# Folding a Fourier transform's first stage into sums and differences of token pairs, in four 64 x 64 float32 products instead of three split products

## The chip, the core and the metric

The kernel runs on one core of one Trainium2 chip. The metric is the device time of one execution in microseconds (us). The engines are TensorE (PE, with its weight loads shown as PEld), VectorE (DVE), ScalarE (ACT), GpSimd (POOL) and SyncE (SP, which here issues nearly all DMA transfers).

## The reference

```python
X = np.fft.rfft(x, axis=1)                       # x: (8, 2496, 256), float32
Y = X * (filt_r + 1j * filt_i)[None]
x = np.fft.irfft(Y, n=2496, axis=1).reshape(8 * 2496, 256)
logits = x @ phi                                 # phi: (256, 32): 8 experts of 4 slots
d = softmax(logits, over all tokens)
slot_input = (d.T @ x).reshape(8, 4, 256)
slot_out = relu(slot_input[e] @ w1[e]) @ w2[e]   # for each expert e, hidden size 1024
out = softmax(logits, over the slots) @ slot_out
```

All eight batches are filtered along their 2496 tokens; then a soft mixture of experts runs over all 19968 tokens together.

## The kernel before

The transform of length 2496 is split as 39 x 64. The **first stage** is a transform of length 39 over tokens that lie 64 apart. Three such groups of tokens stand on 117 partitions of one tile, and two of these sets make a *unit* of 512 columns; a batch has 11 units (`NH`). As a matrix the stage is `w1q`, 117 x 120: cosines and sines for 20 frequencies (`NT`; the other 19 follow by symmetry), for three groups side by side, so that a third of it is not zero. For batch 0 a unit is one float32 matmul (line 323). For batches 1 to 7 the product is split: `split_x` rounds the tokens to the short float kind `float32r` on ACT (line 310, tile `xh`) and takes the remainder on POOL (line 311, `xl`), and `s1_unit` adds three one-pass products, `w1h` by `xh`, `w1l` by `xh` and `w1h` by `xl` (line 327). The result is copied out of PSUM (line 331 on ACT; in batch 0 every second one by line 329 on DVE) to a tile `at` and written to a scratch tensor in HBM, `a_dram`. PSUM has two buffers of one bank for it.

The **second stage** works in *slots*, ten to a batch (`CPB`), 80 in all. `load_ash` brings two frequencies of the scratch back with another order of axes (tile `ash`, five buffers). `x_unit` multiplies by the length-64 transform (line 357, four float32 matmuls) and by the filter tables `ff_t` on DVE and POOL (lines 371 to 375). Two slots later `t_unit` transposes the result (line 383), copies it to `y` on ACT (line 385) and, every second slot, forms the logits in the frequency domain (line 394, strips of 32 columns). Batches are gathered in five groups; when a group is complete, the generator `chain` takes its logits back to tokens and through the soft-max statistics and sums (line 417 and around it), two steps in each slot.

Order: `slot_of` spreads the first-stage units of batches 1 to 7 over 65 slots (`SPAN`), after `EARLY` units that are done before slot 0. In slot n the program issues loads, `split_next(n + 1)` prepares the units of the next slot, `x_unit` runs, then `s1_unit` for this slot's units, then `t_unit` of slot n - 2. A scheduler orders the instructions of each engine from the program's order and priorities; `behind` pins chosen instructions in a queue's written order, among them SP's transfers up to slot 24 (`PIN`). `keep_warm` issues matmuls on zeros during the fill.

After the last slots the last two chains, the experts' layers (lines 910 and 928, strips of 32 columns) and the output products (line 966, strips of 32 rows) follow, and the result is written.

The main loop's order in the code, cut:

```python
for n in range(NS + LT):
    ...
        load_to(n)
        ...
        split_next(n + 1)
        x_unit(*divmod(n, CPB))
    for b, u in at_slot.get(n, ()):
        s1_unit(b, u)
    ...
        t_unit(b, c)
    ...
    hop_slot(n)
```

## Time and profile before

| what | value |
|---|---|
| median of 3 timed runs | 402.03 us (398.9 to 402.43) |
| profiled execution, its own time | 398.26 us |
| its span in the profile | 396.3 us |
| PE busy | 362.1 us, 91% |
| PE weight loads busy | 278.9 us, 70% |
| DVE busy | 264.2 us, 67% |
| ACT busy | 212.6 us, 54% |
| POOL busy | 200.8 us, 51% |
| DMA | 109.08 MB, mean 275 GB/s |

Shares are of the span of one execution. Matmuls are pipelined and float32 matmuls show two records each, so the sum of their durations is more than the time that PE needs; starts of records tell the pace. Lines are named as L327; in a row of groups stand engine, operation, tile written and read, shapes, count, busy time, mean duration and the idle time of the engine before them with what ended it.

### The profile page before, as it was taken

The page shows a single profiled execution, that of the slowest core. Times are in us where ns is not written, and L with a number is a line of the kernel's source. Part 1 is how long each engine was busy: PE and PEld are TensorE (multiplying, and loading weights), DVE is VectorE, ACT ScalarE, POOL GpSimd, SP SyncE. Part 2 cuts the span into 40 slices and gives each one's busy share as a digit, 9 for nine tenths or more (in the row PEclk, how much of TensorE's full clock was granted, in tenths as well). Part 3 has the DMA queues.
Part 4 walks back from the last instruction along what each step waited for, and adds up shares of the span by engine and source line. Part 5 has one row for each costly group of instructions (what it writes and reads, how often), then busy time and mean ns, then how long its engine had stood idle before and what let it go on. Part 6 is the DMA issues. An engine that isn't in the chain of part 4 may idle for free.

```text
span 396.3 us, 11436 instructions
## 1 busy us (share of the span) xinstructions
PE 362.1 (91%) x4569; PEld 278.9 (70%) x4569; DVE 264.2 (67%) x460; ACT 212.6 (54%) x453; POOL 200.8 (51%) x229
## 2 busy tenths in 40 slices
PE   8967889999999999999998999999999899999960
PEld 2455767887878776887887778888767544777850
DVE  1215998779789973967899355899644653588640
ACT  2356656675666946665675634347235431577430
POOL 0157688797668674856774615663421112361000
PEclk9999999999999999999998999999999999999555
DMA  8999999899889866976897783454529998299997
GB/s 293 316 291 368 395 374 373 288 318 341 261 274 305 288 212 207 291 250 171 283 328 215 200 271 104 130 147 134 170 70 380 364 249 278 111 413 421 418 414 296
DMA packets 54010, 109.08 MB, mean 275 GB/s; under 512 B 5362, under 2 KB 25970, under 8 KB 51782
## 3 DMA queue, kind: packets, MB, share of 16 engines
q1 hardware_dynamic: 53412, 108.01, 80.5%
q8 instruction: 36, 0.59, 0.6%
q10 hardware_dynamic: 546, 0.35, 0.3%
q14 instruction: 16, 0.13, 0.1%
HBM read 65.60 MB, written 42.74 MB: 273 GB/s over the span
## 4 chain that ended last, share of the span: by engine, by line
PE 61%; DVE 15%; DMA 13%; ACT 3%; issue 3%; POOL 2%; SPq 1%; DVEq 0%; ACTq 0%; POOLq 0%
PE x L357 14%; PE s L327 9%; PE t L383 7%; DMA out<-ob 5%; PE l L394 4%; PE s L417 4%; DMA ff_t<-in_ff 3%; DMA xt<-in_x 3%; PE v L417 3%; PE dd L417 2%; DVE t L372 2%; PE u L417 2%; PE lg L417 2%; DVE yt L371 2%; DVE yt L374 2%
## 5 line engine op out<-in xcount | busy, mean ns | idle before, releaser
L311 POOL TENSOR_TENSOR xl<-xt,xh 117x512 fp32r<-117x512 f32 x77 | 104.4, 1367 | 37.6 <-ACT xh L310 35.5
L357 PE MATMUL x<-cst_t,ash 128*128 128x128 f32 x640 | 90.2, 281 | 2.9 <-issue 2.3
L357 PEld LDWEIGHTS x<-cst_t,ash 128*128 128x128 f32 x640 | 81.6, 192 | 13.3 <-issue 7.5
L375 POOL TENSOR_TENSOR yt<-yt,t 128x256 f32<-128x256 f32 x80 | 65.4, 818 | 45.5 <-DVE t L372 35.9
L371 DVE TENSOR_TENSOR yt<-x,ff_t 128x512 f32<-128x512 f32 x80 | 54.7, 683 | 27.4 <-PE x L357 25.3
L385 ACT COPY y<-t 128x512 f32<-128x512 f32 x80 | 46.1, 591 | 35.5 <-PE t L383 33.2
L331 ACT COPY at<-s 120x512 f32<-120x512 f32 x83 | 48.5, 587 | 26.2 <-PE s L327 15.1
L310 ACT CAST xh<-xt 117x512 fp32r<-117x512 f32 x77 | 46.3, 623 | 23.4 <-PE s L327 12.6
L372 DVE TENSOR_TENSOR t<-x,ff_t 128x512 f32<-128x512 f32 x80 | 54.2, 678 | 0.0
L383 PE MATMUL t<-cst_t,yt 128*128 128x128 f32 x320 | 48.8, 277 | 4.8 <-POOL yt L375 4.1
L374 DVE TENSOR_TENSOR yt<-yt,t 128x256 f32<-128x256 f32 x60 | 45.3, 766 | 0.8
L383 PEld LDWEIGHTS t<-cst_t,yt 128*128 128x128 f32 x320 | 36.7, 141 | 12.7 <-POOL yt L375 7.2
L327 PE MATMUL s<-xh,w1h 117*120 117x512 f32 x77 | 35.9, 466 | 3.3 <-ACT at L331 2.1
L966 PE MATMUL out<-so,st 32*128 32x256 f32 x468 | 35.6, 337 | 2.0 <-ACT ob L971 1.0
L966 PEld LDWEIGHTS out<-so,st 32*128 32x128 f32 x468 | 30.7, 222 | 6.2 <-ACT ob L971 3.1
L327 PE MATMUL s<-xl,w1h 117*120 117x512 f32 x77 | 31.7, 416 | 0.3 <-POOL xl L311 0.3
L374 POOL TENSOR_TENSOR yt<-yt,t 128x256 f32<-128x256 f32 x20 | 15.1, 754 | 32.6 <-DVE t L372 19.9
L971 DVE COPY ob<-out 128x512 f32<-128x512 f32 (+1 forms) x40 | 25.0, 669 | 8.5 <-DMA out<-ob 5.5
L327 PE MATMUL s<-xh,w1l 117*120 117x512 f32 x77 | 30.4, 395 | 0.0
L971 ACT COPY ob<-out 128x512 f32<-128x512 f32 (+1 forms) x40 | 21.7, 583 | 14.8 <-DMA out<-ob 7.5
L394 PE MATMUL l<-yt,phi_t 128*32 128x128 f32 x640 | 27.5, 280 | 0.1
L394 PEld LDWEIGHTS l<-yt,phi_t 128*32 128x32 f32 x640 | 15.8, 109 | 9.1 <-issue 4.5
(107 smaller groups left out, 474.0 us busy)
## 6 DMA issues: line engine op xcount, KB each, us to landing
ash<-a_dram SPq DMA_DIRECT2D x80, 256.0 KB
a_dram<-at SPq DMA_DIRECT2D x80, 240.0 KB
xt<-in_x SPq DMA_DIRECT2D x35, 512.0 KB
out<-ob SPq DMA_DIRECT2D x17, 1024.0 KB
w<-in_wx SPq DMA_DIRECT2D x42, 256.0 KB
w<-in_wx SPq DMA_DIRECT2D x6, 512.0 KB
x_t<-in_x SPq DMA_DIRECT2D x5, 512.0 KB
ff_t<-in_ff SPq DMA_DIRECT2D x10, 256.0 KB
```

Source lines behind the costliest of these rows:

```text
L311: pool_e.tensor_tensor(out=xl, in0=xs, in1=xh.bitcast(F32), op=ALU.subtract)
L327: pe.matmul(ps, w, xx, start=(n == 0), stop=(n == 2))
L331: act.copy(at, ps)
L357: pe.matmul(ps[:, 2 * k + dh].rearrange("q r c -> q (r c)"), ash[:, k, dh * P : (dh + 1) * P], C("b1" if t0 + k else "b0"), start=True, st ...
L371: dve.tensor_tensor(out=yt, in0=ps, in1=frv, op=ALU.mult)
L372: dve.tensor_tensor(out=t2, in0=ps[:, :, ::-1, :], in1=fiv, op=ALU.mult)
L374: add.tensor_tensor(out=yt[:, :, 1, :], in0=yt[:, :, 1, :], in1=t2[:, :, 1, :], op=ALU.add)
L375: pool_e.tensor_tensor(out=yt[:, :, 0, :], in0=yt[:, :, 0, :], in1=t2[:, :, 0, :], op=ALU.subtract)
L383: pe.transpose(pt[:, k, dh, :], yt[:, c % 2, 2 * k + dh].rearrange("q r c -> q (r c)"), ident)
L394: pe.matmul(pl[32 * j : 32 * j + 32, :], phi_t[:, dh, :], yt[:, j // 2, 2 * (j % 2) + dh].rearrange("q r c -> q (r c)"), start=(dh == 0), ...
L417: line(pe.matmul(*a, **k))
L966: nc.tensor.matmul(prs[k][:, mm, :], sts[n][q, hs, c0 : c0 + P], so[q, ho], start=(i == 0), stop=(i == 2))
```

## The change

The tokens s and 39 - s of a group meet the same cosine and opposite sines. The change has the host lay such pairs side by side (`token_layout`, 19 pairs and the unpaired token 0, 20 rows; three groups on 60 of 64 partitions, and two sets of these on the two halves of the tile), and the kernel forms their sum and difference (`fold_x`, tile `eo`), on POOL for batches 1 to 7 and on DVE for batch 0 and the first two pieces of batch 1. The stage is then a cosine product of the sums and a sine product of the differences, each 64 x 64 for one half of the partitions: four float32 matmuls, one in each quarter of the array, into one PSUM tile of two banks. They get a high priority, so that they stand side by side; so do those of line 394. Work goes in *pieces* (`PIECE`) of two units, one of a single unit first: six to a batch. One copy on ACT takes a piece out of PSUM (two instructions in batch 0, where three pools of PSUM take turns). The scratch has cosine and sine parts as its outer axis, each piece is written by two transfers, and the constants of the second stage are ordered to match (`a1`). The split matrices `w1h` and `w1l`, the cast on ACT and the remainder on POOL are gone. `EARLY` goes from 4 units to 1, the loads of batch 1 move behind batch 0's writes, and the warm-up matmuls are placed anew. The PSUM pool of the stage is closed after its last piece and opened again with two buffers of one bank for the steps behind it.

```diff
@@ -46,8 +46,11 @@
 XC = 4
 XB = 3
-AB = 5
-EARLY = 4
+AB = 4
+EARLY = 1
+PIECE = ((0, 1), (1, 3), (3, 5), (5, 7), (7, 9), (9, 11))
+NU = len(PIECE)
+HR = 20
 SPAN = 65
 ASH = 5
 LT = 2
@@ -55,10 +58,9 @@
 RT = 1
 PR = 2
 FB = 1
-WM = 1
-WK = 2
+WM = 2
+WK = 1
 PIN = 24
-FIRST = (0, 2, 6, 10, 14, 18, 22)
 PA = 6
 YB = 34
 TAIL = (
@@ -73,7 +75,7 @@
 def slot_of(b, u):
-    k = (b - 1) * NH + u - EARLY
+    k = (b - 1) * NH + PIECE[u][1] - 1 - EARLY
     return k * SPAN // ((BATCH - 1) * NH - EARLY) if k >= 0 else -1
@@ -116,20 +118,26 @@
         blocks.append((name, a))
     w1f = w1.reshape(N1, QR)
-    w1q = np.zeros((PK, N1, PK, QR))
+    fold = np.zeros((2, HR, 2, NT))
+    fold[0, :, 0] = w1[0:HR, 0]
+    fold[1, 1:, 1] = w1[1:HR, 1]
+    w1q = np.zeros((2, 64, 2, 64))
     w1d = np.zeros((PK, N1, 2, PK, 2, NT // 2))
     cq = np.zeros((PK, QR, PK, N1))
     for j in range(PK):
-        w1q[j, :, j] = w1f
+        sl = slice(HR * j, HR * j + HR)
+        w1q[:, sl, 0, sl] = fold[0, :, 0]
+        w1q[:, sl, 1, sl] = fold[1, :, 1]
         cq[j, :, j] = w1f.T
         w1d[j, :, :, j] = w1.reshape(N1, 2, 2, NT // 2).transpose(0, 2, 1, 3)
-    w1q = w1q.reshape(KR, QP)
-    put("b0", b0.reshape(P, P))
-    put("b1", b1.reshape(P, P))
+    w1q = w1q.reshape(P, P)
+    put("b0", b0.transpose(1, 0, 2, 3).reshape(P, P))
+    put("a1", b1.transpose(1, 0, 2, 3).reshape(P, P))
     put("id", np.eye(P))
     put("sgn", sgn.reshape(NT // 2, P))
     put("m0", inverse(bh))
     put("m1", inverse(b1))
+    put("b1", b1.reshape(P, P))
     put("bh", bh.reshape(P, P))
     put("w1d", w1d.reshape(KR, 2 * PK * NT))
     put("cq", cq.reshape(QP, KR))
@@ -229,17 +242,14 @@
     const = ctx.enter_context(tc.tile_pool(name="const", bufs=1))
     scr = ctx.enter_context(tc.tile_pool(name="scr", bufs=3, space=DRAM))
-    ps_s1 = ctx.enter_context(tc.tile_pool(name="ps_s1", bufs=2, space=PSUM))
     ps_x = ctx.enter_context(tc.tile_pool(name="ps_x", bufs=2, space=PSUM))
     ps_t = ctx.enter_context(tc.tile_pool(name="ps_t", bufs=2, space=PSUM))
     ps_c = ctx.enter_context(tc.tile_pool(name="ps_c", bufs=2, space=PSUM))
-
-    w1q_t = const.tile([KR, QP], F32, name="w1q_t")
-    act.dma_start(w1q_t, w1q)
-    w1h = const.tile([KR, QP], F32R, name="w1h")
-    w1l = const.tile([KR, QP], F32R, name="w1l")
-    nc.vector.tensor_copy(w1h, w1q_t)
-    nc.vector.tensor_tensor(out=w1l, in0=w1q_t, in1=w1h.bitcast(F32), op=ALU.subtract)
+    ps_s1_cm = tc.tile_pool(name="ps_s1", bufs=1, space=PSUM)
+    ps_s1 = [ps_s1_cm.__enter__()]
+
+    w1q_t = const.tile([P, 2, 64], F32, name="w1q_t")
+    act.dma_start(w1q_t.rearrange("q c m -> q (c m)"), w1q)
     cst_t = const.tile([P, CST.shape[1]], F32, name="cst_t")
     phi_t = const.tile([P, 2, SLOTS], F32, name="phi_t")
@@ -285,56 +295,66 @@
         if pinned[0]:
             behind("sp", ins)
-    def keep_warm(n):
+    def keep_warm(n, w=512):
         for k in range(n):
-            behind("pe", pe.matmul(pw, warm[:, 0:P], warm, start=True, stop=True))
+            behind("pe", pe.matmul(pw[:, 0:w], warm[:, 0:P], warm[:, 0:w], start=True, stop=True))
     def load_x(b, c):
-        t = proda.tile([P, XC, DIM], F32, tag="xt", name=f"xt{b}_{c}", bufs=XB)
-        i0 = c * XC
-        n = min(XC, NI - i0)
-        issue(t[:, 0:n, :], x[b, :, i0 : i0 + n, :])
+        t = proda.tile([P, 2, 2, DIM], F32, tag="xt", name=f"xt{b}_{c}", bufs=XB)
+        lo, hi = PIECE[c]
+        issue(t[:, 0 : hi - lo].rearrange("q u a d -> q (u a) d"), x[b, :, 2 * lo : 2 * hi, :])
         xts[b, c] = t
-    xhl = {}
-
-    def split_x(b, u):
-
-        if b < FB:
-            xhl[b, u] = x0_t[0:KR, 2 * u : 2 * u + 2, :], None
-            return
-        c, k = divmod(2 * u, XC)
-        xs = xts[b, c][0:KR, k : k + 2, :]
-        xh = proda.tile([KR, 2, DIM], F32R, tag="xh", name=f"xh{b}_{u}", bufs=3)
-        xl = proda.tile([KR, 2, DIM], F32R, tag="xl", name=f"xl{b}_{u}", bufs=3)
-        act.copy(xh, xs)
-        pool_e.tensor_tensor(out=xl, in0=xs, in1=xh.bitcast(F32), op=ALU.subtract)
-        xhl[b, u] = xh, xl
+    eos = {}
+
+    def fold_x(b, u):
+
+        lo, hi = PIECE[u]
+        n = hi - lo
+        xs = x0_t[:, lo:hi] if b < FB else xts.pop((b, u))[:, 0:n]
+        eo = proda.tile([P, 2, 2, DIM], F32, tag="eo", name=f"eo{b}_{u}", bufs=2)
+        eng = dve if b < FB or (b, u) < (1, 2) else pool_e
+        eng.tensor_tensor(out=eo[:, 0, 0:n], in0=xs[:, :, 0], in1=xs[:, :, 1], op=ALU.add)
+        eng.tensor_tensor(out=eo[:, 1, 0:n], in0=xs[:, :, 0], in1=xs[:, :, 1], op=ALU.subtract)
+        eos[b, u] = eo
     a_dram = {}
     def s1_unit(b, u):
         if u == 0:
-            a_dram[b] = scr.tile([N2, QR, DIM], F32, tag="a_dram", name=f"a_dram{b}")
-        xh, xl = xhl.pop((b, u))
-        ps = ps_s1.tile([QP, 2, DIM], F32, tag="s1", name=f"s1_{b}_{u}")
-        if xl is None:
-            at = ypool.tile([QP, 2, DIM], F32, tag="y", name=f"at{b}_{u}")
-            behind("pe", pe.matmul(ps, w1q_t, xh, start=True, stop=True))
+            a_dram[b] = scr.tile([2, N2, NT, DIM], F32, tag="a_dram", name=f"a_dram{b}")
+        lo, hi = PIECE[u]
+        n = hi - lo
+        eo = eos.pop((b, u))
+        pool, tag = ((ps_s1[0], "s1"), (ps_x, "x"), (ps_t, "t"))[u % 3 if b < FB else 0]
+        if tag == "s1":
+            both = pool.tile([P, 2, 2, DIM], F32, tag=tag, name=f"s1_{b}_{u}")
+            pss = [both[:, r] for r in range(2)]
         else:
-            at = proda.tile([QP, 2, DIM], F32, tag="at", name=f"at{b}_{u}", bufs=AB)
-            for n, (w, xx) in enumerate(((w1h, xh), (w1l, xh), (w1h, xl))):
-                pe.matmul(ps, w, xx, start=(n == 0), stop=(n == 2))
-        if b == 0 and u % 2 == 1:
-            dve.tensor_copy(at, ps)
+            pss = [pool.tile([P, 2, DIM], F32, tag=tag, name=f"s1_{b}_{u}_{r}") for r in range(2)]
+        with tc.high_priority():
+            for c, r in ((1, 0), (1, 1), (0, 0), (0, 1)):
+                q = slice(64 * r, 64 * r + 64)
+                ps = pss[r][64 * c : 64 * c + 64, 0:n]
+                ins = pe.matmul(ps, w1q_t[q, c], eo[q, c, 0:n], start=True, stop=True)
+                if b < FB or (b, u) < (1, 2):
+                    behind("pe", ins)
+        at = proda.tile([P, 2, 2, DIM], F32, tag="at", name=f"at{b}_{u}", bufs=AB)
+        if tag == "s1" and b >= FB:
+            act.copy(at[:, 0:n], both[:, :, 0:n].rearrange("q r u d -> q u r d"))
         else:
-            act.copy(at, ps)
-        k0 = PK * 2 * u
-        if u < NH - 1:
-            issue(a_dram[b][k0 : k0 + 2 * PK].rearrange("(i j) q d -> (j q) i d", j=PK), at)
-        else:
-            issue(a_dram[b][k0 : k0 + PK].rearrange("j q d -> (j q) d"), at[:, 0, :])
-            issue(a_dram[b][k0 + PK], at[0:QR, 1, :])
+            for r in range(2):
+                copy = dve.tensor_copy if u == NU - 1 and r else act.copy
+                copy(at[:, 0:n, r], pss[r][:, 0:n])
+        ka, kb = 2 * PK * lo, min(2 * PK * hi, N2 - N2 % PK)
+        for c in range(2):
+            issue(
+                a_dram[b][c, ka:kb].rearrange("(m j) t d -> (j t) m d", j=PK),
+                at[64 * c : 64 * c + PK * HR, 0:n].rearrange("q u r d -> q (u r) d")[:, 0 : (kb - ka) // PK],
+            )
+        if hi == NH:
+            for c in range(2):
+                issue(a_dram[b][c, N2 - 1], at[64 * c : 64 * c + HR, n - 1, 1])
     ys = {}
     lts = {}
@@ -345,7 +365,7 @@
         t0 = 2 * c
         ash = prod.tile([P, 2, DIM], F32, tag="ash", name=f"ash{b}_{c}", bufs=ASH)
         ashs[b, c] = ash
-        issue(ash, a_dram[b].rearrange("k (r t) d -> (k r) t d", t=NT)[:, t0 : t0 + 2, :])
+        issue(ash, a_dram[b].rearrange("r k t d -> (r k) t d")[:, t0 : t0 + 2, :])
     def x_unit(b, c):
@@ -354,13 +374,15 @@
         ps = ps_x.tile([P, 4, 2, 64], F32, tag="x", name=f"x_{b}_{c}")
         for k in range(2):
             for dh in range(2):
-                pe.matmul(
+                ins = pe.matmul(
                     ps[:, 2 * k + dh].rearrange("q r c -> q (r c)"),
                     ash[:, k, dh * P : (dh + 1) * P],
-                    C("b1" if t0 + k else "b0"),
+                    C("a1" if t0 + k else "b0"),
                     start=True,
                     stop=True,
                 )
+                if (b, c) == (0, 0):
+                    behind("pe", ins)
         frv, fiv = (
             ff_t[:, c, k].rearrange("q (p o c) -> q p o c", o=1, c=64).broadcast_to([P, 4, 2, 64]) for k in range(2)
         )
@@ -389,15 +411,16 @@
+            with tc.high_priority():
...
@@ -665,9 +688,10 @@
     CPB = NT // 2
     NS = BATCH * CPB
-    units = [(b, u) for b in range(1, BATCH) for u in range(NH)]
+    units = [(b, u) for b in range(1, BATCH) for u in range(NU)]
+    NEARLY = sum(hi <= EARLY for _, hi in PIECE)
     at_slot = {}
-    for b, u in units[EARLY:]:
+    for b, u in units[NEARLY:]:
         at_slot.setdefault(slot_of(b, u), []).append((b, u))
     xnext = [(b, c) for b in range(1, BATCH) for c in range(6)]
@@ -678,13 +702,12 @@
     def split_next(n):
         for b, u in at_slot.get(n, ()):
-            split_x(b, u)
-            if u % 2 == 1 or u == NH - 1:
-                next_x()
-
-    x0_t = x0p.tile([P, NI, DIM], F32, name="x0_t")
-    for i0, i1 in zip(FIRST, FIRST[1:]):
-        issue(x0_t[:, i0:i1], x[0, :, i0:i1])
+            fold_x(b, u)
+            next_x()
+
+    x0_t = x0p.tile([P, NH, 2, DIM], F32, name="x0_t")
+    for lo, hi in PIECE:
+        issue(x0_t[:, lo:hi].rearrange("q u a d -> q (u a) d"), x[0, :, 2 * lo : 2 * hi])
     warm = ypool.tile([P, 512], F32, tag="y", name="warm")
     dve.memset(warm, 0.0)
     first = ypool.tile([P, 2], F32, tag="y", name="first")
@@ -694,16 +717,14 @@
     keep_warm(WM)
     tabs_next = iter(range(CPB))
-    split_x(0, 0)
-    for u in range(NH):
-        if u + 1 < NH:
-            split_x(0, u + 1)
+    fold_x(0, 0)
+    for u in range(NU):
+        if u + 1 < NU:
+            fold_x(0, u + 1)
         s1_unit(0, u)
-        if u in (3, 7):
-            next_x()
+        if u == 1:
+            tc.keep_in_program_order(act.dma_start(cst_t[:, 0:NEAR], cst[:, 0:NEAR]))
         if u == 2:
-            tc.keep_in_program_order(act.dma_start(cst_t[:, 0:NEAR], cst[:, 0:NEAR]))
-        if u == 4:
             tc.keep_in_program_order(act.dma_start(phi_t, phi.rearrange("(h q) e -> q h e", q=P)))
     x0_cm.__exit__(None, None, None)
     work_cm, work = open_pool("work", 1, "left")
@@ -712,22 +733,24 @@
     def load_to(n):
         while loads:
             b, c = loads[0]
-            if n < max(b * CPB + c - (3 if b < 2 else ASH), slot_of(b, NH - 1) + 2 if b else -3):
+            if n < max(b * CPB + c - (3 if b < 2 else ASH), slot_of(b, NU - 1) + 2 if b else -3):
                 break
             load_ash(*loads.pop(0))
     keep_warm(WK)
+    load_tables(next(tabs_next))
     next_x()
-    load_tables(next(tabs_next))
+    next_x()
     load_to(-3)
     load_tables(next(tabs_next))
+    load_to(-2)
+    next_x()
+    load_to(-1)
     make_signs()
-    for u in range(EARLY):
-        split_x(1, u)
+    for u in range(NEARLY):
+        fold_x(1, u)
         s1_unit(1, u)
-        if u % 2 == 1:
-            next_x()
-            load_to(-2 + u // 2)
+    keep_warm(WK)
     sign_tables(0)
     split_next(0)
     late = list(tabs_next)
@@ -795,6 +818,8 @@
             s1_unit(b, u)
         if n == last_s1:
             proda_cm.__exit__(None, None, None)
+            ps_s1_cm.__exit__(None, None, None)
+            ps_s1[0] = ctx.enter_context(tc.tile_pool(name="ps_s2", bufs=2, space=PSUM))
             late_cm, lp = open_pool("late", WL, "right")
             work2_cm, lp2 = open_pool("work2", 1, "left")
             late_pool.extend((lp, lp2))
```

More of the change, by code (lines that the diff above doesn't have):

```diff
@@ L194, in token_layout @@
 def token_layout(x):
[L196 to L199 removed]
+    rows = np.zeros((BATCH, 2, 64, NH, 2, DIM), x.dtype)
+    for u in range(NH):
+        for k in range(PK * 2 * u, min(PK * 2 * (u + 1), N2)):
+            r, j = divmod(k - PK * 2 * u, PK)
+            for s in range(HR):
+                rows[:, r, HR * j + s, u, 0] = x[:, token_of(s, k)]
+                if s:
+                    rows[:, r, HR * j + s, u, 1] = x[:, token_of(N1 - s, k)]
+    return rows.reshape(BATCH, P, NI, DIM)
 def out_place(m):
```

28 lines of the change are left out of this document (12 added, 16 removed).

## The prediction

> **What bounds the kernel now.** I read the table of stages first (the span cut where the work changes), then the stages with the first stage's matmuls alone, then the costliest groups, then single rows of the chain and of the timeline for prices. The columns of the stage table are the stretch in us, its length, the busy time of PE, weight load, DVE, ACT and POOL, the granted clock, the share of the DMA engines and GB/s.
>
> ```profile
> 0.00:28.00 28.00, 23.16 (x63) 10.78 (x64) 4.88 (x10) 11.60 (x21) 6.66 (x10) 1.00 0.90 302
> 28.00:62.00 34.00, 28.71 (x228) 22.21 (x229) 26.75 (x38) 20.53 (x41) 26.05 (x23) 1.00 1.03 374
> 62.00:89.00 27.00, 26.39 (x242) 21.76 (x242) 21.29 (x35) 18.13 (x38) 24.01 (x23) 1.00 0.94 320
> 89.00:235.00 146.00, 141.46 (x1895) 114.09 (x1895) 112.56 (x178) 94.10 (x195) 95.05 (x87) 0.99 0.82 259
> 120.00:140.00 20.00, 19.14 (x327) 16.37 (x326) 19.93 (x29) 15.78 (x36) 14.54 (x14) 1.00 0.87 285
> 200.00:220.00 20.00, 17.66 (x298) 15.33 (x297) 19.33 (x29) 13.05 (x30) 12.62 (x12) 0.91 0.81 251
> ```
>
> Up to 28 us the kernel fills; from 28 to 62 the DMA engines are full (1.03, 374 GB/s) and PE has holes. From 62 on PE is busy 26.39 of 27 and 141.46 of 146 us, so there the next thing to do waits for PE. Two limits stand close behind: POOL with 24.01 of 27 in the third row, and DVE with 19.93 and 19.33 of 20 in the two cut-outs, where a chain of soft-max steps runs. After 235 no first-stage matmul is left:
>
> ```profile
> 28.00:62.00 34.00, 13.98 (x42) 6.74 (x42) 1.00 1.03 374
> 62.00:89.00 27.00, 11.64 (x33) 5.23 (x33) 1.00 0.94 320
> 89.00:235.00 146.00, 42.95 (x142) 23.51 (x142) 0.99 0.82 259
> 235.00:290.00 55.00, 0.00 (x0) 0.00 (x0) 1.00 0.50 150
> ```
>
> These are the records of line 327 alone, three to a unit of two token groups: 14 units between 28 and 62, 11 between 62 and 89, 47 between 89 and 235, and the other 5 before 28. Only the 58 units of the two PE-bound stages can turn PE time into time.
>
> **The change part by part.** *PE, what goes.* A unit is three matmuls of 512 columns. The chain of waits gives the price of a pair of units, and the timeline how the pair stands between its neighbours:
>
> ```profile
> 199.21 1.39 PE s L327 x6
> 193.29 0.89 PE x L357 x8
> 196.70 1.09 PE x L357 x8
> 196.12 0.57 PE l L394 x16
> 326.75 1.85 PE h L910 x16
> 198.96 0.48 PE L327 MATMUL s<-xh,w1h 117*120 117x512 f32 x1
> 200.44 1.04 PE L383 MATMUL t<-cst_t,yt 128*128 128x128 f32 x8
> ```
>
> Six matmuls take 1.39 us, 0.23 each, and with the exposed first weight load a pair holds PE from 198.96 to 200.44, 1.48 us.
>
> *PE, what comes.* A piece of two units is four float32 matmuls of 64 rows by 64 columns, 512 moving columns each; float32 shows two records to a matmul. One record of 128 columns at full width costs 0.89/8 = 0.111 us (the row at 193.29), so one of 512 costs 0.445, and four matmuls in a row would cost 8 x 0.445 = 3.56 us. But rows of before show products in different strips of the array running together. Line 910 has four strips of 32 columns: 16 records of 512 columns in 1.85 us, where one after another they would take 7.1, that is 3.85 at a time. For strips of rows the nearest row is the output stage:
>
> ```profile
> 347.07 2.03 PE L966 MATMUL out<-so,st 32*128 32x256 f32 x37
> 199.28 0.39 PE L327 MATMUL s<-xh,w1l 117*120 117x512 f32 x1
> 199.51 0.39 PE L327 MATMUL s<-xl,w1h 117*120 117x512 f32 x1
> ```
>
> A one-pass matmul of 512 columns costs 0.23 (start to start, the last two rows), so one of 256 some 0.115; 37 of them in 2.03 us are 2.1 at a time. Two row strips at a time by two column strips make the four quarters stream together, as one of line 910's sets of eight records does: 1.85/2 = 0.925 us. The other end is 2.1 at a time in all, 1.70 us. I take 0.925: each direction has a row with at least as many strips at once as is needed, though no row has both directions in one matmul.
>
> Entering and leaving this narrow form costs too. After the narrow line 394 the next eight records of line 357 take 1.09 us instead of 0.89, so leaving costs 0.20. Line 394 itself holds 0.57 where 16 records four at a time would need 16 x 0.111/4 = 0.44, so its entry costs about 0.1, of which 0.925 holds a part already. Between 1.10 and 1.25 for a piece I take **1.15**. Pair against piece: 1.48 - 1.15 = 0.33 us, 0.165 a unit. A single unit (0.23 x 3 + 0.09 = 0.78 now) becomes 0.46 + 0.25 = 0.71, about nothing, and there is one in eleven.
>
> The Trainium skill (TensorEngine Tiling (Array Packing), Tiling Modes, Key Properties) says that changing the tiling mode drains the engine, which speaks against 42 such pieces among full-width work; this trace agrees with its 1.09 against 0.89. Without that rule a piece would be 0.925 and the pair would give 0.55.
>
> *PE, the sum.* 47 units x 0.165 = 7.8 us between 89 and 235, and 11 x 0.165 = 1.8 between 62 and 89. In the two cut-outs (40 of the 146 us) DVE is full and nothing is gained: 7.8 x 40/146 = 2.1 is taken off. **7.5 us** are left.
>
> *ACT and POOL.* These rows are the groups before, with busy time, mean ns and idle time before them:
>
> ```profile
> L311 POOL TENSOR_TENSOR xl<-xt,xh 117x512 fp32r<-117x512 f32 x77 | 104.4, 1367 | 37.6 <-ACT xh L310 35.5
> L331 ACT COPY at<-s 120x512 f32<-120x512 f32 x83 | 48.5, 587 | 26.2 <-PE s L327 15.1
> L310 ACT CAST xh<-xt 117x512 fp32r<-117x512 f32 x77 | 46.3, 623 | 23.4 <-PE s L327 12.6
> L401 ACT COPY lt<-l 128x128 f32<-128x128 f32 x40 | 10.8, 269 | 15.5 <-PE l L394 15.0
> L327 PE MATMUL s<-xh,w1h 117*120 117x512 f32 x77 | 35.9, 466 | 3.3 <-ACT at L331 2.1
> L371 DVE TENSOR_TENSOR yt<-x,ff_t 128x512 f32<-128x512 f32 x80 | 54.7, 683 | 27.4 <-PE x L357 25.3
> ```
>
> The cast of line 310 goes (46.3 us of ACT), and two copies of 587 become one of 1024 elements, 0.587 + 512 x (0.587 - 0.269)/384 = 1.01 us. ACT loses some 50 us, but it is busy 94.10 of 146 where PE is full, so its own time is worth nothing; the waits before line 327 that it caused are 3.3 us in all. I count them at nothing, because another wait takes their place: the fold is two instructions of 512 elements for a piece, 2 x 1.367 = 2.73 us on POOL, after which the matmuls may start, where a single unit now waits 0.623 + 1.367 = 1.99 us. POOL's total stays (77 instructions of 512 elements before, sums and differences of as many after, but for three units' that go to DVE), but it comes in runs of 2.7 us, and line 375's subtraction queues behind them on POOL, and the transposes of line 383 behind that. Two slots lie between a subtraction and its transposes. Line 357 has eight records to a slot:
>
> ```profile
> 62.00:89.00 27.00, 10.90 (x84) 10.50 (x84) 1.00 0.94 320
> ```
>
> That is 10.5 slots in 27 us, 2.6 us each, so the run of 2.73 is covered, with little to spare.
>
> *PSUM.* The stage has one tile of two banks instead of two of one. The next piece's matmuls wait for the copy of 1.01 us. With 65 slots for the 41 pieces behind the early one, at 2.6 us a slot, pieces are 4.1 us apart; it costs nothing unless two pieces are set side by side, and then about 1 us.
>
> *DMA.* Bytes are the same (512 KB in and 480 KB out for a pair). The write of a piece is two transfers instead of two for two units, so SP's queue issues 14 writes a batch against 12 beside the ten `ash` loads, some 0.33 us each by the row at 24.07 below: 0.7 us in a batch of 27, and nothing.
>
> *The start.* Batch 0 is folded on DVE: two instructions of 0.683 for each of five pieces and a half, 7.5 us on an engine that is busy 4.88 of the first 28. The lead on batch 1 shrinks from four units to one, and two `xt` loads leave the midst of batch 0's writes:
>
> ```profile
> 11.72 0.61 SPq L284 DMA_DIRECT2D xt<-in_x  x1
> 16.30 0.68 SPq L284 DMA_DIRECT2D xt<-in_x  x1
> 24.07 0.33 SPq L284 DMA_DIRECT2D ash<-a_dram  x1
> ```
>
> Three units that are not done ahead are 3 x 496 KB = 1.49 MB less before the first slots, 4.0 us at the 374 GB/s of the full stage. They are done later, where they cost 3 x 0.58 = 1.7 us of PE. Batch 1's last piece now falls into slot 7 and its first load into slot 9, for use in slot 10: a copy of 1.01, a write, and a load have under three slots, and a wait of 1 to 2 us there is likely. I keep **1.5 us**, between -1 and 4.
>
> *The end.* Everything behind 235 us moves as a block: weight loads start when buffers come free, the output stage is untouched. Nothing is gained or lost. The higher priority of line 394's matmuls changes nothing either: the row at 196.12 has all 16 side by side already. The other order of the rows in `b0` and `a1` changes no instruction, and the warm-up matmuls (four for three) lie in the fill.
>
> Sum: 7.5 + 1.5 = 9.0 us. The profiled execution took 398.26 (span 396.3), so it would be 389.3. The three timed runs were 398.9, 402.03 and 402.43, up to 4 us above it; I set **390** for the changed kernel.
>
> **The rivals.**
>
> *The gain is swallowed (20%).* DVE needs 112.56 of 146 us and POOL 24.01 of 27 now. If PE's faster stretches only bring the chain's DVE steps and the fold's runs on POOL to the front, the units in the DVE-bound stretches gain nothing and the others lose half to waits on POOL: 9.6/2 - 2.1 + 0 at the start, 2.7 us, or 396 to 401. For it speaks that 62:89 has POOL at 89% already, so that stage can't fall under 24; against it that ACT's 12.6 us of waits and its cast are gone from the path.
>
> *All of it lands (10%).* Form changes that stand beside line 394's share its drain, and line 327's waits of 3.3 us go: 58 units x 0.23 = 13.3, with 4 us at the start 17: 381.
>
> *Slower: the quarters do not stream four at a time (15%).* Place: every piece, on PE. If two quarters at a time is all that the array does, or if the two records of each product stay in a row so that a quarter waits for the one before, the change does not do what it says. A piece is then 1.70 + 0.25 = 1.95 us against 1.48, 0.47 more for 29 pieces in the two PE-bound stages: +13.6, less the 1.5 of the start: 410. It decides from where the streaming takes over 1.48 - 0.25 = 1.23 us, that is 3.56/1.23 = 2.9 quarters at a time. Line 966's 2.1 speaks for it, line 910's 3.85 against. The Trainium skill (TensorE: Matmul & The Clock Gate, Measured speedup vs the span model) says that tiles of rows and columns compose, with about 4 ns for each more; no run here shows quarters, and by that page a piece would stream in hardly more than one matmul's time, as I chose.
>
> *Forecast (55%)*: 384 to 396.
>
> **How the numbers follow.** A measurement of this kernel can tell about 1% from no change, so faster means under 398 and slower over 406. Faster: 0.55 and 0.10, and a third of the swallowed case, 0.71. Slower: the 0.15 of the third rival, nearly all of it over 406, so 0.14. The rest, 0.15, is no change. The range leaves out the top of the slower rival and the bottom of the full gain: 379 to 407.
>
> **What would show it.** Right: the four quarters of a piece start within some 10 ns, twice, 0.43 us apart; a piece holds PE for 1.1 to 1.2 us from its first start to the next work; the first `ash` load is issued before 24.07; no unit's matmuls wait long for POOL. Wrong: quarters 0.43 apart one by one; PE idle in front of the pieces with POOL as the releaser; DVE over 19 of 20 in more stretches than two; a hole in PE at slot 10.

## The result and the profile after

The changed kernel takes **411.0 us** (median of four, 410.04 to 411.9) where the kernel before takes 400.46 on the same chip: a ratio of **1.034, 95% interval 1.0265 to 1.0415**. The ratio counts executions in the fast state alone (of the kernel before 396.03 and 398.9), which is why it is more than 411.0 / 400.46. The change is slower; 390 was predicted, and 411 lies above the range of 379 to 407. The profiled execution took 410.04, with a span of 408.2.

The stages of the changed kernel, in the columns of the stage table of before:

```profile
0.00:28.00 28.00, 18.61 (x91) 7.86 (x92) 11.27 (x21) 9.14 (x17) 0.20 (x4) 0.91 0.88 306
28.00:62.00 34.00, 26.26 (x239) 16.80 (x238) 27.10 (x39) 12.71 (x20) 26.02 (x24) 0.95 0.89 305
62.00:89.00 27.00, 24.06 (x221) 16.42 (x220) 15.62 (x27) 9.54 (x16) 16.69 (x18) 0.91 0.95 309
89.00:235.00 146.00, 137.75 (x1863) 93.42 (x1860) 104.49 (x176) 69.56 (x124) 104.74 (x97) 0.99 0.87 279
235.00:290.00 55.00, 54.40 (x946) 44.88 (x945) 41.61 (x75) 24.96 (x54) 24.92 (x34) 1.00 0.40 115
```

From 28 to 62 us the DMA engines, full before (1.03, 374 GB/s), run at 0.89 and 305. PE, busy 26.39 of 27 us from 62 to 89 before, is busy 24.06, at a clock of 0.91. The engine that was to be relieved has more holes. The page's groups of the changed lines, then what PE waited for in all (us, times, longest), after and before, the small waits left out:

```profile
L317 POOL TENSOR_TENSOR eo<-xt 128x512 f32<-128x512 f32 (+1 forms) x40 | 48.9, 1223 | 50.8 <-DMA xt<-in_x 42.2
L339 PE MATMUL s<-eo,w1q_t 64*64 64x512 f32 (+1 forms) x384 | 55.4, 604 | 14.2 <-DVE eo L318 6.5
L344 ACT COPY at<-s 128x1024 f32<-128x1024 f32 (+1 forms) x42 | 39.6, 942 | 63.6 <-PE s L339 36.0
```

```profile
PE s L339 <- DVE eo L318: 6.5, 6, 4.8
PE t L405 <- POOL yt L397: 5.8, 7, 1.4
PE s L339 <- POOL eo L318: 4.8, 7, 2.0
PE x L377 <- DMA ash<-a_dram: 3.6, 3, 1.8
PE s L339 <- ACT at L344: 2.7, 2, 2.4
```

```profile
PE t L383 <- POOL yt L375: 4.1, 4, 1.8
...
PE s L327 <- ACT at L331: 2.1, 2, 1.9
```

POOL stood idle 42.2 us for loads of tokens ahead of the fold (line 317), PE waited for the fold, and where line 327 had 3.3 us of idle time before it, line 339 has 14.2. Line 339 does batch 0 as well: the 6.5 us for DVE's fold all lie before slot 0, 4.8 of them in one wait. In the main loop PE waited 4.8 us for POOL's fold, and 2.7 for the copy that frees the stage's one PSUM tile.

The stretches of the main loop show where the time went. The numbers are the starts of the first matmul of `x_unit` in slots 0, 10, 20, 60 and 79, and of the first output product, in the two traces, rounded to 0.1 us before they are subtracted:

| stretch | before | after | difference | predicted |
|---|---|---|---|---|
| start to slot 0 | 27.9 | 26.4 | -1.5 | -1.5 |
| slots 0 to 10 | 33.9 | 34.7 | +0.8 | 0 |
| slots 10 to 20 | 26.8 | 30.7 | +3.9 | -1.8 |
| slots 20 to 60 | 146.0 | 152.2 | +6.2 | -5.7 |
| slots 60 to 79 | 52.2 | 52.3 | +0.1 | 0 |
| slot 79 to the outputs | 54.4 | 56.9 | +2.5 | 0 |
| outputs to the end | 55.1 | 55.0 | -0.1 | 0 |
| span | 396.3 | 408.2 | +11.9 | -9.0 |

Three stretches hold the miss of 21 us: slots 10 to 20, slots 20 to 60, and the tail.

Was the price of a piece wrong? The chain of waits of the changed kernel, first a usual piece, then one of two that were broken up:

```profile
164.14 0.44 PE t L405 x4
164.57 1.02 PE s L339 x8
165.59 0.48 PE t L405 x3
...
157.09 1.00 PE s L339 x2
158.09 0.34 PE l L417 x2
158.43 1.00 PE s L339 x2
159.43 0.34 PE l L417 x2
159.76 1.00 PE s L339 x2
160.76 0.34 PE l L417 x2
161.10 1.00 PE s L339 x2
```

Eight records, four products, in 1.02 us: the four quarters do stream together. In the rows of the single records the four start at 164.504, .511, .517 and .524, and the second four 0.48 us later. 40 of 42 pieces look so. In the other two, logits matmuls, which also have the high priority, stepped between the quarters. In the one shown each quarter took 1.00 us alone, and it holds PE 5.0 us; in the other, at 146 us, three quarters ran together and the fourth alone.

### The profile page after: what moved, and what is told of

Same layout as the page of the kernel before. It is cut to its first block, busy times and chain, and to the rows that moved or that the text cites. A ratio compares the mean times of both kernels' runs of the same rounds, so it can differ in the third digit from the quotient of the medians.

```text
span 408.2 us, 11555 instructions
## 1 busy us (share of the span) xinstructions
PE 363.9 (89%) x4702; PEld 256.8 (63%) x4702; DVE 261.1 (64%) x470; ACT 174.6 (43%) x346; POOL 197.8 (48%) x232
## 4 chain that ended last, share of the span: by engine, by line
PE 51%; DVE 6%; ACT 2%; DMA 2%; issue 1%; POOL 1%; DVEq 0%; ACTq 0%; POOLq 0%
PE x L377 9%; PE out L991 7%; PE s L339 5%; PE t L405 5%; PE s L440 5%; PE l L417 3%; PE dd L440 3%; PE lg L440 2%; PE u L440 2%; PE h L935 2%; PE o L953 2%; DMA ash<-a_dram 2%; DVE ob L996 1%; PE v L440 1%; PE v L437 1%
## 5 line engine op out<-in xcount | busy, mean ns | idle before, releaser
L393 DVE TENSOR_TENSOR yt<-x,ff_t 128x512 f32<-128x512 f32 x80 | 54.7, 684 | 54.8 <-PE x L377 30.6
L397 POOL TENSOR_TENSOR yt<-yt,t 128x256 f32<-128x256 f32 x80 | 68.2, 855 | 44.4 <-DVE t L394 41.5
L317 POOL TENSOR_TENSOR eo<-xt 128x512 f32<-128x512 f32 (+1 forms) x40 | 48.9, 1223 | 50.8 <-DMA xt<-in_x 42.2
L339 PE MATMUL s<-eo,w1q_t 64*64 64x512 f32 (+1 forms) x384 | 55.4, 604 | 14.2 <-DVE eo L318 6.5
L344 ACT COPY at<-s 128x1024 f32<-128x1024 f32 (+1 forms) x42 | 39.6, 942 | 63.6 <-PE s L339 36.0
L405 PE MATMUL t<-cst_t,yt 128*128 128x128 f32 x320 | 51.3, 280 | 5.9 <-POOL yt L397 5.8
L318 POOL TENSOR_TENSOR eo<-xt 128x512 f32<-128x512 f32 (+1 forms) x40 | 50.8, 1271 | 0.0
L396 DVE TENSOR_TENSOR yt<-yt,t 128x256 f32<-128x256 f32 x60 | 38.1, 643 | 0.9
L991 PEld LDWEIGHTS out<-so,st 32*128 32x128 f32 x468 | 34.0, 265 | 3.2 <-DVE ob L996 1.5
L396 POOL TENSOR_TENSOR yt<-yt,t 128x256 f32<-128x256 f32 x20 | 15.1, 753 | 32.1 <-DVE t L394 16.1
L417 PE MATMUL l<-yt,phi_t 128*32 128x128 f32 x640 | 29.3, 282 | 0.0
L339 PEld LDWEIGHTS s<-eo,w1q_t 64*64 64x64 f32 x384 | 11.2, 137 | 28.0 <-DVE eo L318 8.8
L440 PE MATMUL s<-y,dd 128*32 128x256 f32 x320 | 20.9, 381 | 0.2 <-ACT dd L596 0.2
```

What stands on the lines that cost most here:

```text
L318: eng.tensor_tensor(out=eo[:, 1, 0:n], in0=xs[:, :, 0], in1=xs[:, :, 1], op=ALU.subtract)
L339: ins = pe.matmul(ps, w1q_t[q, c], eo[q, c, 0:n], start=True, stop=True)
L393: dve.tensor_tensor(out=yt, in0=ps, in1=frv, op=ALU.mult)
L396: add.tensor_tensor(out=yt[:, :, 1, :], in0=yt[:, :, 1, :], in1=t2[:, :, 1, :], op=ALU.add)
L397: pool_e.tensor_tensor(out=yt[:, :, 0, :], in0=yt[:, :, 0, :], in1=t2[:, :, 0, :], op=ALU.subtract)
L405: pe.transpose(pt[:, k, dh, :], yt[:, c % 2, 2 * k + dh].rearrange("q r c -> q (r c)"), ident)
```

## The experiments

The time of each is its median; the ratio is to the kernel before on the same chip, with its 95% interval. Where a run is set against the changed kernel, 411.0 is meant. The runs were made on several chips, on which the kernel before had medians from 399.0 to 401.0, and stretches are read from one profiled execution of each; a difference of 1 to 2 us between runs is therefore not shown by itself.

**Is PE time of the first stage worth time at all?** In the kernel before, one of three products is left out:

```diff
-for n, (w, xx) in enumerate(((w1h, xh), (w1l, xh), (w1h, xl))):
-    pe.matmul(ps, w, xx, start=(n == 0), stop=(n == 2))
+for n, (w, xx) in enumerate(((w1h, xh), (w1h, xl))):
+    pe.matmul(ps, w, xx, start=(n == 0), stop=(n == 1))
```

> The kernel before with the middle one of line 327's three products left out for batches 1 to 7 (that part of the computation is missing); casts, remainders, copies and transfers stay. It takes 0.23 us of PE from every unit and changes nothing else, so it asks whether PE time of the first stage is worth time in the old kernel at all. If PE is the bound from 62 to 235 us, as the prediction had it: 11 x 0.23 + 47 x 0.23 x 106/146 = 10.4 us, 389 to 391. If waits elsewhere (transfers, POOL, the chain on DVE) come up at once, as the runs with the changed kernel suggest: 1 to 5 us, 395 to 400.

Measured: 391.82, ratio 0.985 (0.978 to 0.991). Slots 20 to 60 took 139.3 us instead of 146.0, so 6.7 of the 10.9 us taken from PE there came through. Slots 0 to 20 took 60.6 as against 60.7: nothing of the 5.8 us (25 units) taken there. The stage table of this run:

```profile
28.00:62.00 34.00, 29.94 (x219) 23.83 (x218) 27.56 (x39) 21.07 (x42) 25.31 (x23) 0.85 1.03 375
62.00:89.00 27.00, 24.86 (x232) 19.93 (x231) 21.89 (x34) 17.67 (x37) 23.63 (x23) 1.00 0.90 295
89.00:235.00 146.00, 137.97 (x1963) 111.27 (x1963) 120.19 (x190) 95.03 (x200) 99.19 (x94) 0.99 0.84 273
```

In 28 to 62 the granted clock was 0.85 in this run, so the plain case is the second row, at full clock. In 62 to 89 PE's busy time fell from 26.39 to 24.86 and nothing came sooner: a PE that is busy 26.39 of 27 us was not the bound there. From 89 on it was, for two thirds of what it was relieved of.

The same question put to the changed kernel, with work added in slots 0 to 19:

```diff
-        for k in range(2):
+        for k in (0, 0, 1) if b < 2 else (0, 1):
```

> The changed kernel with two of the four second-stage matmuls of line 377 done twice in slots 0 to 19, 20 x 0.45 = 8.9 us more of PE time where the prediction had 62 to 89 us bound by PE. If PE's work bounds these slots: +7 to +9 us, 418 to 420. If waits bound them and PE's thinner work lets the clock fall to one half: between -3 and +3, 408 to 414, and fewer half-clock stretches before 130 us.

Measured: 413.76, ratio 1.037 (1.029 to 1.045): 8.9 us more of PE work cost 2.8, and slot 20 starts 2.4 us later. In the changed kernel too most of these slots' time is bound by something else.

**The fold on POOL.** The products of batches 1 to 7 read the tokens as they come, so their sums and differences are left out:

```diff
         xs = x0_t[:, lo:hi] if b < FB else xts.pop((b, u))[:, 0:n]
+        if (b, u) >= (1, 2):
+            eos[b, u] = xs.rearrange("q n a d -> q a n d")
+            return
```

> The changed kernel without the sums and differences of batches 1 to 7 (all but the two early pieces): the quarters read the loaded tokens as they are, so POOL loses 100 us of work and no piece waits for it. Theory A (the fold's delay on POOL, which also holds back the subtraction of line 397): PE's waits for eo and for yt go, the half-clock stretches between 28 and 150 us go with them, and the time is 390 to 397. Theory B (order) and C (the quarters' own price): 405 to 410, since both stay.

Measured: 402.5, ratio 1.010 (1.006 to 1.013). 8.5 of the 11 us are gone; slots 20 to 60 take 146.8. PE's waits for POOL's subtraction (line 397) fell from 5.8 to 1.5 us and those for POOL's fold went, and 6.3 us of waits for loads of tokens came in. This is the largest single effect found, and it still isn't faster than before.

**The loads ahead of the fold.** The changed kernel keeps two loads of tokens under way; with a third:

```diff
         s1_unit(1, u)
+        next_x()
     keep_warm(WK)
```

> One more load of tokens is issued behind the early piece, so that three xt tiles are on their way instead of two, as in the kernel before. Theory A (the stage is starved: POOL waits 45 us for xt loads, and PE behind it): those waits fall under 20 us, PE's waits for eo from 11 us to under 4, and the time goes from 411 to some 404. Theory B (order: quarters and strips of other stages are mixed by the two priorities): 408 at best, only because no piece happens to be broken up in this order. Theory C (the price of 42 pieces with their changes of form): 411.

Measured: 408.19, ratio 1.020 (1.013 to 1.027), 2.8 us better. What the engines of the fold (POOL, and DVE for two pieces) waited for, in the changed kernel and in this one (us, times):

```profile
  DMA xt<-in_x: 45.4, 11
```

```profile
  DMA xt<-in_x: 16.1, 10
```

29 us less waiting there gave 2.8 us. PE's waits for the fold did not fall under 4 us, as theory A had it; between 25 and 150 us those on POOL rose, again in the changed kernel and in this one:

```profile
PE s L339 <- POOL eo L318: 4.3, 5, 2.0
```

```profile
PE s L339 <- POOL eo L318: 10.3, 10, 2.1
```

So POOL's idle time is no measure of what the pieces waited for. One more load, a fold one slot earlier, three buffers of `eo` and four of `xt`:

```diff
-XB = 3
+XB = 4
...
-        eo = proda.tile([P, 2, 2, DIM], F32, tag="eo", name=f"eo{b}_{u}", bufs=2)
+        eo = proda.tile([P, 2, 2, DIM], F32, tag="eo", name=f"eo{b}_{u}", bufs=3)
...
-            split_next(n + 1)
+            split_next(n + 2)
```

> Sums and differences are formed two slots ahead of their products instead of one, with three eo tiles and four xt tiles, and two more loads go ahead of the slots. Theory A: PE's waits for eo (11 us) fall under 3 and the time to 398 to 403. Theory B and C: 407 to 411, with PE's waits gone but no time won.

Measured: 407.65, ratio 1.022 (1.013 to 1.031). Slots 10 to 20 fell to 23.9 us, 2.9 below before and more than predicted; slots 0 to 10 rose to 38.9 and the rest took it back. The wait moved; it did not go.

**The lead.** Pieces done early, one or three (`EARLY` 1 or 5), with the third load:

```diff
-EARLY = 1
+EARLY = 5
```

> Three pieces of batch 1 (five units) are done before slot 0 instead of one, each followed by a load of the next tokens, so the x loads are also three deep. Theory A: the hole before slot 10 (6.6 us between two x_units) closes, slots 0 to 20 take 60 to 62 us instead of 65.4, and the time is 399 to 402; the start is 2 to 3 us later. Theory B: like x_depth, 406 to 409, since some pieces are broken up here too. Theory C: 411.

Measured: 415.71, ratio 1.039 (1.031 to 1.048): worse. Against the run with one early piece and the third load, slot 0 starts 2.9 us later and slot 20 9.3 us later. And the old kernel with half its lead:

```diff
-EARLY = 4
+EARLY = 2
```

> The kernel before with a lead of two units instead of four. Theory A in its part on the lead: slots 10 to 20 take 29 to 31 us instead of 26.8, with PE waits and a half-clock stretch, and the time is 404 to 408. If the lead does not matter: 399 to 402.

Measured: 399.9, ratio 1.000 (0.996 to 1.004). A shorter lead by itself costs the old kernel nothing.

**The priorities.** Line 394's logits with the high priority in the old kernel, without it in the new, and neither line with it:

```diff
+            with tc.high_priority():
                 for dh in range(2):
```

> The kernel before with the high priority for the logits matmuls of line 394 alone. Theory B (that priority breaks up the strips of other stages): the sums s<-y,dd stream 9.5 us or more between slots 20 and 60 instead of 8.3, the tail from the last slot to the output takes 56 to 57 us instead of 54.5, and the time is 404 to 407. Theory A and C: 399 to 402.

> Line 394's logits matmuls (line 417 there) lose the high priority, the quarters keep it. Theory B: no piece is broken up any more (two are in the changed kernel, at some 5 us together), and the sums s<-y,dd need 8.3 to 8.8 us of PE streaming in the middle stage and the tail each instead of 10.5 and 10.2; time 403 to 406. Theory A: 409 to 411, the waits of POOL for xt stay over 35 us. Theory C: 411.

> Neither the quarters nor the logits matmuls have a high priority. Theory B: three pieces are broken up by other matmuls, each at 2 to 4 us, but the strips of the sums are not: 406 to 411. Theory A: 409 to 412. If the priority moved pieces ahead of ready work (PE waiting for eo), those waits fall from 11 us to under 5 and the time by as much.

Measured: 399.34 in the old kernel (0.997, 0.993 to 1.002), 410.27 in the new without it (1.025, 1.019 to 1.032), and 418.22 without both (1.041, 1.031 to 1.051). So the logits' priority costs next to nothing in time; without that of the pieces too some 8 us are lost. In that run six of the 42 pieces (three were expected) stand in two parts, and the last batch's pieces stand within a slot of their plan; which of the two costs the time is not shown. The records do show a price of the logits' priority on PE: the 320 records of the soft-max sums (line 417 before, 440 after), four strips of columns, start in 82 groups in the old kernel, 98 with the priority added, 100 in the changed kernel and 82 there without it. The chain of waits, before and after:

```profile
288.25 4.45 PE s L417 x80
```

```profile
297.82 2.86 PE s L440 x49
300.68 0.11 PE l L417
300.79 0.18 PE s L440 x3
300.97 0.33 PE l L417 x11
301.30 0.10 PE s L440
301.39 0.01 PE l L417 x2
301.41 1.54 PE s L440 x25
```

Eighteen groups more at 0.21 us are 3.8 us of PE, and taking them away, and the two broken pieces with them, gave 0.7. Other waits took their place, the longest of them on the copy out of PSUM: in the changed kernel without the logits' priority (`l_plain`) one piece stands right behind another and waits for the copy that frees the one PSUM tile, while ACT's queue works on the soft-max chain ahead of that copy:

```profile
PE s L339 <- ACT at L344: 5.0, 1, 5.0
```

No run gave the stage a second PSUM tile, so what this tile costs is not shown.

**Pieces running ahead.** With their priority the pieces of the last batch stand at slots 44 to 49, planned for 55 to 64. Tied, in order alone, behind the last matmul of their slot's `x_unit` (with the third load, the logits plain):

```diff
                     behind("pe", ins)
+                elif "slot" in queue:
+                    after_slot(ins)
...
+                queue["slot"] = ins
```

> On top of the third x load: the logits without priority, and each piece is tied behind the second-stage matmuls of its own slot, so that it can't be pulled ahead (in the changed kernel the last batch's pieces stand 15 slots ahead of their plan, in the kernel before 4 to 6). No piece is broken up. Theory D (pieces pulled ahead wait at the head of PE's queue for a fold that is not there, and bring loads forward): PE's waits for eo between slots 20 and 60 fall from 5 us to under 2, and the time to 395 to 400. Theory A without D (latency of load and fold alone): more waits, as pieces have less lead: 408 to 414.

> The first of these with two pieces (three units) done ahead instead of one. Theory A in its part on the lead: the hole before slot 10 shrinks from 6 us to 3, no half clock at 60 us, 2 to 4 us faster than the tie alone. If the lead does not matter, as in the kernel before with two units: equal to the tie alone or 1 to 2 us slower by the later start.

Measured: 409.58 (1.025, 1.019 to 1.030), and with a lead of three units 406.43 (1.017, 1.012 to 1.022). The tie alone won nothing: against the third load alone, slots 20 to 60 fell from 148.5 to 147.2 us and slots 10 to 20 rose from 30.6 to 34.1. In the planned order two units more of lead are worth 3.2 us, and here, with the whole computation, the stretch with the largest miss is no longer behind: slots 20 to 79 take 197.9 us, where the kernel before takes 198.2. Nearly all that is lost then stands ahead of slot 20, which starts at 95.6 instead of 88.6. The same tie on the early fold gave 411.71 (1.030, 1.022 to 1.038).

**SP's queue.** Most transfers are issued by SP in one order, and one that waits holds all behind it. SP's waits between 28 and 95 us, before and after:

```profile
SPq L284 <- PE x L357: 6.7, 9, 2.1
SPq L284 <- POOL xl L311: 5.8, 4, 4.0
...
SPq L284 <- ACT at L331: 3.4, 5, 1.8
```

```profile
SPq L294 <- ACT at L344: 9.6, 5, 5.6
```

SP's waits in all are no longer than before, where it waited up to 4.0 us for POOL; what is new is that a piece's write waits for its copy up to 5.6 us, with the loads behind it. In the next run ACT itself issues the writes (with the third load), and in the one after all is joined to order and lead:

```diff
-    def issue(dst, src):
+    def issue(dst, src, q=None):
+        if q is not None:
+            q.dma_start(dst, src)
+            return
...
+                act if b >= FB else None,
```

> The kernel with the third x load, and the writes of the pieces of batches 1 to 7 issued by ACT, right behind its copy, instead of SP. Theory E (SP's written order: its queue waits 12 to 15 us between 20 and 100 us for a piece's copy, with loads queued behind it, and the DMA engines move 305 to 331 GB/s between 28 and 60 us against 373 in the kernel before): those waits go, 350 GB/s or more in that stretch, slot 20 is reached some 4 us earlier, and the time is 401 to 405 (from 408.2). If the queue is not it: 407 to 410.

> The kernel with the tie to slots and a lead of three units (406.4), with its writes issued by ACT. Theory E: PE's 9.3 us of waits for ash between 25 and 150 us fall under 4, the half-clock stretches at 65 and 89 us go, and the time is 398 to 402. Else 405 to 408.

Measured: 407.08 (1.017, 1.012 to 1.022) and **405.56** (1.015, 1.010 to 1.019), the lowest median of those that compute all, though its interval overlaps that of the same version with SP's writes. The waits for the copy to `at` leave SP; those for the writes to land grow instead, from 7.4 us with the third load alone to 17.6 in the first of these runs (20 to 100 us). Slot 20 starts at 87.6 in the second run, before the old kernel's 88.6. Slots 20 to 60 give it back, 151.4 against 146.0 before and 144.4 with SP's writes. The timeline of the second run (start, us, in brackets the idle time before and what ended it) shows one place:

```profile
135.63 3.18 ACTq L299 DMA_DIRECT2D a_dram<-at  x2
...
139.14 1.15 ACT L588 COPY u<-u 128x240 f32<-128x240 f32 x4 [3.54 <-DMA a_dram<-at]
139.81 1.47 PE L450 MATMUL u<-cst_t,d 117*32 117x60 f32 x48 [6.89 <-ACT u L588]
```

Two writes held ACT's queue for 3.18 us, a copy of the soft-max chain waited behind them, and PE stood still for 6.89. With SP's writes the same wait of PE is there with 4.6 us, so what ACT's writes added at this place is some 2.3 us; for the rest of the 7.0 us between the two runs no cause is shown. Part of the price of the waiting write moved from SP's queue to ACT's.

Do the causes add up? The same without the fold:

> The changed kernel with the writes of pieces issued by ACT, the lead of three units, pieces tied to their slots, three loads of tokens under way, and without the sums and differences for batches 1 to 7 (that part of the computation is missing: the products read the tokens). If the causes found so far (fold on POOL, loads, order of SP's queue, lead) add up, 405.6 less the 8.5 that the fold alone was worth: 396 to 398, below the kernel before. If they are the same loss seen from several sides, or if the soft-max chain in slots 20 to 40 and the tail set the rest, 401 to 404.

Measured: 404.58, ratio 1.014 (1.006 to 1.022). They do not, and the run brings in a wait of its own: without the fold the matmuls, not POOL, set the buffer of tokens free, and SP's next load waits for them, between 40 and 95 us

```profile
SPq L301 <- PE s L349: 17.6, 6, 5.2
```

so it can't tell the fold's share in that order. Its slots 20 to 60 take 145.1, 0.9 us below the old kernel's and no less than the 144.4 of the same order with the fold and with SP's writes; the loss stands in slots 10 to 20 (30.8) and before slot 0 (30.7).

**The clock.** The changed kernel has the granted clock lower early; here PEclk of the pages, before and after:

```profile
PEclk9999999999999999999998999999999999999555
```

```profile
PEclk9969997999999989999999999999999899995555
```

Ahead of the output stage the clock is halved for 3.4 us before and for 20.5 after, in stretches of 3.4 or 6.8 us. In these two traces each of the five halvings follows a window of 3.4 us in which PE streams, by the starts of its records, for 0.00 to 0.39 of the time. The bound is not sharp: in the other runs a few halvings follow windows of up to 0.55, and some windows of 0.34 to 0.39, one of them in the changed kernel's fill, are followed by none. The work that falls into halved stretches would stream in some 2 us before and 8 to 10 after at full clock, so the lower clock costs at most some 8 us. The Trainium skill (TensorE: Matmul & The Clock Gate, Part 1) has the same window of about 3.4 us and the same half clock; the records agree. Is the clock a cause, or does it follow the waits? Five full-width matmuls fill the hole ahead of slot 10:

```diff
+        if (b, c) == (1, 0):
+            pw2 = ps_c.tile([P, 512], F32, tag="c", name="warm_hole")
+            for _ in range(5):
+                behind("pe", pe.matmul(pw2, warm[:, 0:P], warm, start=True, stop=True))
```

> The changed kernel with five warm-up matmuls of zeros, 4.3 us, put between the second-stage matmuls of slot 9 and slot 10, where PE now waits for the ash load and the clock falls to one half for 6.8 us behind it. Theory F (each 3.4 us window that PE fills less than about 0.4 costs a stretch at half clock, and that is most of the loss): no half clock between 55 and 75 us, slots 10 to 20 take 27 to 28 us instead of 30.7, and the time falls by 2 to 3 us. If the clock costs nothing because the loads bound these slots: +0 to +3 us.

```profile
L377 PE MATMUL warm_hole<-warm x10: 592/592/595, 54.9 to 58.7; 128*128 128x512 f32 x10
```

Measured: 412.38, ratio 1.030 (1.026 to 1.034). The ten records ran in the hole, the halving at 60 us went, and another came at 87; slots 10 to 20 took 33.6 us where they had taken 30.7. At this place the clock followed the waits and cost nothing of its own that could be won.

In the tail it is otherwise. Of the 15 runs with the changed kernel, the eight whose clock stays full between slot 79 and the outputs take 53.9 to 55.5 us there; the three with a halved stretch of 3.4 us, the changed kernel among them, take 56.4 to 56.9, and the four with one of 6.8 us take 57.7 to 58.8. Each of these halvings follows a window in which PE streams for 0.15 to 0.55 of the time, and how much of the loss is this thin work and how much the clock behind it is not told apart.

## Why the prediction was wrong

**The price of a piece held.** Four quarters at a time, as taken from line 910; 1.02 us and about 0.1 of entry against 1.15. Worked out from the starts of PE's records, the first stage in slots 20 to 60 held PE for some 36.1 us for 47 units before (30.2 of streaming, 5.9 between records), 0.77 each, and for some 32.4 us for 52 units after (26.2, 1.1, and 5.1 for some 50 more changes of form), 0.62 each, with the two broken pieces in it. 0.15 a unit was saved against 0.165 predicted. So the slower rival named the time, 410, by luck, for a reason that is not there: its condition, fewer than 2.9 quarters at a time, is false in 40 pieces of 42.

**The step that failed most is the wait for the fold.** The prediction set it against the waits that go ("I count them at nothing, because another wait takes their place") and saw it as 2.73 us on POOL against 1.99, "covered, with little to spare". Without the fold 8.5 us are gone, where this step had put nothing. The 2.73 are POOL's work once the tokens are there, and the change also gives each fold a whole piece to wait for while two loads are under way: 42.2 us of POOL's idle time at line 317 is for tokens, against 4.6 for tokens on ACT at line 310 before. That depth of the loads is only a part: the third load is worth 2.8 us, and PE waited longer for POOL with it (10.3 us against 4.3). How the 8.5 divide between POOL's work on the fold, the subtraction that queues behind it and the loads is not shown.

The other wait that "costs nothing" in the prediction is that for the one PSUM tile, unless two pieces stand side by side, "and then about 1 us". The wait for the copy cost PE 2.7 us in the changed kernel, not far from the 2.1 of before with two tiles, but 5.0 in `l_plain`.

**The second is that "from 62 on" PE is busy, "so there the next thing to do waits for PE".** For 62 to 89 it was wrong: with 0.23 us taken from each unit of the old kernel, slots 10 to 20 did not move (26.8 and 26.7). The term of 1.8 us was never there to be had. That stage's DMA share is 0.94 and its POOL is at 24.01 of 27; which of these bound it was not tested.

For slots 20 to 60 the premise was right in kind: two thirds of the time taken from PE came through, where I had counted 106/146. But the saving was used up: five more units fell there (some 3 us, from the lead given up and from pieces pulled forward), waits of more than 0.3 us rose from 5.7 to 8.7 us, one broken piece took some 3.6 more, and the sums and logits, cut up by the priority, took 3 more. These counts overlap, and how much of the 6.2 us each carries is not shown singly. In the planned order with a lead of three units the 6.2 us were gone, but the 5.7 predicted did not come: 0.3 us were won from slot 20 to 79.

**The start** came as predicted to slot 0 (-1.5), though by the prediction's own terms (4.0 less 1.7 less 1 to 2) it was 0.3 to 1.3. The price of the lost lead came further on: in the changed kernel two units of lead are worth 3.2 us once pieces stay in their slots; in the old kernel they are worth nothing (`EARLY` 2: 1.000). The wait forecast at slot 10 is there, 1.57 us for `ash` right after 1.98 us for a fold; five matmuls filled these holes without moving the slot (61.15 and 61.1).

**That the higher priority of line 394 "changes nothing"** held in time (0.997 in the old kernel, 0.7 us in the new), not in mechanism: it cuts other groups of strips.

**"Everything behind 235 us moves as a block"** held for slots 60 to 79 and the outputs and missed 2.5 us between them. The chain of waits shows a hole, and the clock halved behind it; first the same steps before, then after:

```profile
305.89 1.44 PE lg L417 x4
307.33 1.30 PE dd L417 x6
```

```profile
312.31 1.11 issue
...
315.49 0.70 DVE v L503
316.19 0.04 issue
316.24 2.67 PE lg L440 x4
318.91 1.77 PE dd L440 x6
```

In the eight runs of the changed kernel without the halved stretch the tail was 53.9 to 55.5 us, close to the old 54.5: so the loss goes with the hole and the halving, not with the tail's own work.

**Swallowed**, the rival at 20%, had the right kind of mechanism, half its gain lost to waits on POOL, but its top was 401; nothing in it made waits cost more than PE could win.

**What stays open.** No version with the whole computation came nearer than 405.56, 1.5% above before. Why slots 10 to 20 still take 28.7 and 30.8 us in the two runs without the fold was not settled, and a second PSUM tile was not tried; the runs show that waits replace each other (fold, loads, the copy out of PSUM, SP's order, ACT's queue), and `all_three` that their effects can't be added.

## What to carry to other kernels

A busy share near one does not show that an engine is the bound: take a known piece of its work away in the old kernel first, as `two_products` did, and see in which stage time follows. When an operation is made to wait for larger pieces of input, count the loads that are under way and the buffers behind it, not only the instructions, and follow each write that waits through the queue that issues it. An idle engine ahead of the operation is not yet a loss: look at whether the engine behind it waits less when the idle time goes. A step that costs "nothing" because it is "covered, with little to spare" is where the range has to open upward.

## What the runs showed of the hardware

- Four float32 products of 64 rows by 64 columns run at the same time if they stand side by side: starts 7 ns apart, 1.02 us for 512 columns each. With a product of another form between them each takes 1.00 us by itself.
- A change of form costs about 0.1 us between starts: the last record of line 405 stands 0.203 us ahead of the first quarter, where 0.109 lies between its own records. In slots 20 to 60 PE changes form 63 times before and 115 times after.
- The engine whose queue issues a transfer can stand still for it: 3.18 us on ACT for two writes of a piece.
- A half clock of 3.4 us in the tail goes with 1 to 3 us more there, one of 6.8 us with 2 to 5 us (runs of the changed kernel, one profile each).
